# Delta-rule attention and MoE on one core: T K left out, transposes by halves of the rows, v and T straight beside crossed keys

## The chip, the cores and the metric

The kernel runs on one core of a Trainium2 chip. The metric is the device time of one execution in microseconds (us). Three runs of the kernel before took 693.31, 692.15 and 690.77 us; the median is 692.15.

## What is computed

The inputs are q, k and v (4 batches, 8 heads, 768 tokens, 48 numbers each), beta, and the weights of a two-layer MoE. Attention runs through the tokens with a state of 48 x 48 for each batch and head; its output, all heads of a token side by side (384 numbers), goes through the MoE. All is fp32.

```
for t in range(S):
    y[:, :, t] = einsum('bhd,bhde->bhe', q[:, :, t], state)
    v_old = einsum('bhde,bhd->bhe', state, kt)
    state = state + beta_t * einsum('bhd,bhe->bhde', kt, vt - v_old)
...
h = maximum(x @ w_in, 0)
out = (h * h) @ w_out
```

kt is k divided by its norm.

## The kernel before

**Units.** A unit is 128 tokens of two batches: two chunks (c) of 64 tokens, eight heads (h, as pairs p with j = 0 or 1 in a pair), two batches (b). There are 12 units (u). A tile has 128 partitions, 64 for each batch. Within a chunk the recurrence is solved in one go: with the products of keys K K' below the diagonal and beta a triangular matrix is inverted, and the inverse is T. If V and K are the chunk's values and keys and S the state before it, the chunk's update is U = T (V - K S). The state becomes S + K' U, and the output is Q S plus the masked products Q K' times U.

**Crosswise layout.** `load_to` (line 226) puts k, q and v so that the even heads of batch b lie in partition half b and the odd heads in the other half. `load_beta` lays beta in the same way (line 256). An operation on one half of the partitions then uses one half of TensorE's rows, and where the result lies sets the half of its columns: four quadrants of the array, which can work side by side.

**Stages of a unit.**
- `normalize`: k divided by its norm (ScalarE L273, VectorE L274 to L286).
- `static`: k and q are transposed on TensorE (L317, four 128x128 transposes for each chunk and each of k and q) and copied to `kq` by ScalarE (L318); products of keys with keys and queries (L327), masked by VectorE (L336); the key products go through DRAM into a layout for the inverse (`lt`).
- `invert`: 31 steps of two VectorE instructions (L415, L416) on `lt`, then DMAs through DRAM into `tt` (T) and `t1t`.
- `whole`: T's remaining quarter (L454, L462, copies L456, L466). Then, for both chunks, T K (L474), which is copied over the keys in `kq` (L483), and T V (L481), copied over `vt` (L484).
- `sequential`, for each chunk: (T K) S and Q S (L505), U = T V - (T K) S on VectorE (L508), K' U into the state (L518, L521), masked products times U (L526), copy of y (L529).
- `moe`: y is transposed (L541, three 128x128 for each chunk), split into a high part x_h (ScalarE, L543) and a low part x_l (VectorE, L544). Each product is made of three: high by high, high by low, low by high. First layer L574 into a PSUM bank `h` (nine matmuls make a step), activation L581, L582, cast L584 (h_h), low part on VectorE L553 (h_l); second layer L561 (six matmuls make a step) two groups behind the first.

**The order.** The code writes each engine's order itself. `weave` (line 613) interleaves the parts of one round by places between 0 and 1: the MoE of unit u-1 is the filler (34 steps), and between its steps come `static` of unit u+1, the state part (`whole` and `sequential`) of unit u in 7 steps from 0.34 to 0.98, the inverse of unit u+1, loads and norms. Each `yield` in a stage ends a step. Every engine takes its instructions in that order. The split of the weights into halves (`split_weights`) runs at the start and within unit 1.

**PSUM.** `ps_x` has two banks (transposes, products, T's parts, state updates), `ps_g` a pair of banks (chunk 1 of `static`, T V, the outputs of `sequential`), `ps_h` two (first layer, and the transposes of y), `ps_o` two (second layer).

Of the kernel before, what the change touches and what calls it, by code (L numbers as in the profile page):

```python
# [20 lines left out]
def kernel(  # L21
# [204 lines left out]
    def load_to(dst, x, d, width, queues=None):  # L226

        for j, queue in enumerate(queues or (nc.sync, nc.sync)):
            for b, src in enumerate(tokens(x, d)):
                rows = slice((b ^ j) * C, (b ^ j) * C + C)  # L230
                for c in range(NC):
                    queue.dma_start(out=dst[rows, c, j::2, :width], in_=src[:, c, j::2])

    def load(u):
        t0, b0 = (u // NU) * P, (u % NU) * 2
        d = dict(u=u, t0=t0, b0=b0, y=[None] * NC, marks={})
# [9 lines left out]
    def load_beta(d):  # L246
# [49 lines left out]
    def static(d):  # L296
# [15 lines left out]
        def transposed(c, which, bank=None):  # L312

            src = d["qp" if which else "kp"]
            tp = (x_tile(u) if bank is None else bank).rearrange("p (n t) -> p n t", n=NP)
            for p in range(NP):
                nc.tensor.transpose(tp[:, p], src[:, c, 2 * p:2 * p + 2].rearrange("p a b -> p (a b)"), ident)  # L317
            return lambda: nc.scalar.copy(out=kq[:, c, :, :, which], in_=tp.rearrange("p n (b t) -> p n b t", b=2))  # L318

        def products(c, first, n):  # L320

            ps = [x[:, :NP * n * C].rearrange("p (n t) -> p n t", n=NP) for x in banks(c)]
            for p in range(NP):
                for j in range(2):
                    rows = slice(j * C, j * C + D)
                    for b in range(2):
                        nc.tensor.matmul(ps[j][b * C:(b + 1) * C, p], lhsT=kq[rows, c, p, b, 0],  # L327
                                         rhs=kq[rows, c, p, b, first:first + n].rearrange("p x t -> p (x t)"),
                                         start=True, stop=True)
# [24 lines left out]
        if u <= 1:  # L354
            for c in range(NC):
                transposed(c, 0)()
                yield
# [7 lines left out]
            for c in range(NC):  # L365
                transposed(c, 1)()
                yield
# [9 lines left out]
        for copy in [transposed(c, which, bank) for c in range(NC) for which, bank in enumerate(banks(c))]:  # L377
            copy()
# [60 lines left out]
    def whole(d):  # L439

        u, ap, kp, vt, kq = (d[x] for x in ("u", "ap", "kp", "vt", "kq"))
# [26 lines left out]
        ps = [x_tile(u).rearrange("p (c n t) -> p c n t", c=NC, n=NP) for _ in range(2)]  # L468
        for c in range(NC):
            for h in range(H):  # L470
                p, j = h // 2, h % 2
                for b in range(2):
                    rows = slice(b * C, (b + 1) * C)
                    nc.tensor.matmul(ps[b][j * C:(j + 1) * C, c, p], lhsT=kp[rows, c, h], rhs=tt[rows, c, h],  # L474
                                     start=True, stop=True)
        g = ps_g.tile([P, 2, PC], F32, name="g")[:, :, :H * D].rearrange("p c (h e) -> p c h e", h=H)
        for c in range(NC):
            for h in range(H):
                for b in range(2):
                    rows = slice(b * C, (b + 1) * C)  # L480
                    nc.tensor.matmul(g[rows, c, h], lhsT=tt[rows, c, h], rhs=vt[rows, c, h], start=True, stop=True)  # L481
        for b in range(2):
            nc.scalar.copy(out=kq[:, :, :, b, 0], in_=ps[b])  # L483
        nc.scalar.copy(out=vt, in_=g)  # L484
        yield


    def sequential(d):
        u, s = d["u"], state[d["u"] % NU]
        kq, ap, kp, vt = (d[x] for x in ("kq", "ap", "kp", "vt"))  # L490
        for c in range(NC):
# [4 lines left out]
            if first:  # L496
                uu = vt[:, c]
            else:
# [267 lines left out]
```

## Time and profile before

| | |
|---|---|
| span of the profiled execution | 691.8 us |
| its place beside the runs | median of three runs 692.15 us, 0.35 above that span |
| TensorE matmuls (PE) | 628.9 us busy, 91% |
| weight loads (PEld, beside the matmuls) | 583.2 us, 84% |
| VectorE (DVE) | 433.1 us, 63% |
| ScalarE (ACT) | 332.8 us, 48% |
| GpSimd (POOL) | 76.4 us, 11% |
| DMA | 49.95 MB, 72 GB/s on average |

In the profile's rows a name such as `x<-tt,kpad` reads: written tile, then what is read, the moving operand ahead of the stationary one. A shape "64*64 64x48" is the weights' rows and columns, then the output. Busy times of matmuls are longer than the pace at which they follow each other, because they overlap; the pace is the difference of two start times. L numbers are lines of the kernel before; in the changed kernel the same statements stand some lines further down (L574 becomes L581, L561 L568, L553 L560, L317 L324, L327 L340, L505 L498, L518 L520, L526 L528, L481 L509, L508 L501, L541 L545, L544 L551, L415 and L416 L429 and L430).

### The profile page before, as it was taken

The numbers are of one execution on the slowest core, as the hardware profiler recorded it, in microseconds if no ns is written. First come the engines' busy times: TensorE is split into PE (matmuls) and PEld (weight loads), VectorE is DVE, ScalarE is ACT, GpSimd is POOL, SyncE is SP. The second block draws the span as 40 slices with busy tenths as digits, with TensorE's granted clock in tenths as the row PEclk, the third lists the DMA queues.
The fourth block names the chain that finished last, engine by engine and source line by source line (L and its number), as shares of the span: only waits on it lengthen the run. The fifth ranks groups of instructions, "written<-read, shape, count | busy, mean of one in ns | idle before, by whom it ended". The sixth has DMA issues, their size and how long they took to land.

```text
span 691.8 us, 23593 instructions
## 1 busy us (share of the span) xinstructions
PE 628.9 (91%) x10084; PEld 583.2 (84%) x10084; DVE 433.1 (63%) x1175; ACT 332.8 (48%) x632; POOL 76.4 (11%) x94
## 2 busy tenths in 40 slices
PE   1740797889999999999999999999999999999997
PEld 0530366779999999999999999999999999999997
DVE  3789776898468387477485494694674775641221
ACT  3630455763453544544535535535545445354352
POOL 8540332310100100001001001001000010000000
PEclk9985689999999999999999999999999999999999
DMA  7678620410441531532423414405315324030100
GB/s 158 158 207 290 195 48 5 91 24 2 89 81 20 103 67 23 107 55 39 96 48 55 99 28 77 90 17 114 65 18 107 58 36 97 3 61 3 24 2 23
DMA packets 174712, 49.95 MB, mean 72 GB/s; under 512 B 166400, under 2 KB 169488, under 8 KB 174608
## 3 DMA queue, kind: packets, MB, share of 16 engines
q1 hardware_dynamic: 172016, 47.85, 32.4%
q8 instruction: 79, 1.29, 0.8%
q10 hardware_dynamic: 2336, 0.59, 0.4%
q14 instruction: 25, 0.20, 0.1%
q0 software_dynamic: 256, 0.01, 0.1%
HBM read 37.32 MB, written 11.01 MB: 70 GB/s over the span
## 4 chain that ended last, share of the span: by engine, by line
PE 78%; DVE 4%; ACT 1%; issue 1%; DVEq 0%
PE h L574 30%; PE o L561 29%; PE g L505 3%; PE g L481 3%; PE x L518 2%; PE x L474 2%; PE x L327 2%; PE g L526 1%; PE g L327 1%; PE g L317 1%; PE x L317 1%; PE h L541 1%; PE x L462 1%; PE x L454 1%; DVE tmp L415 1%
## 5 line engine op out<-in xcount | busy, mean ns | idle before, releaser
L561 PE MATMUL o<-w,h_h 128*128 128x384 f32 x768 | 203.7, 346 | 0.0
L574 PE MATMUL h<-x_h,w 128*128 128x256 f32 x1152 | 173.4, 286 | 1.7 <-ACT x_h L543 1.7
L574 PEld LDWEIGHTS h<-x_h,w 128*128 128x128 f32 x1152 | 153.6, 189 | 7.3 <-ACT x_h L543 2.0
L553 DVE TENSOR_TENSOR h_l<-r,h_h 128x512 fp32r<-128x512 f32 x96 | 66.6, 694 | 147.9 <-PE o L561 61.5
L581 ACT ACTIVATE r<-h 128x512 f32<-128x512 f32 x96 | 57.5, 599 | 179.0 <-PE h L574 178.7
L561 PEld LDWEIGHTS o<-w,h_h 128*128 128x128 f32 x768 | 133.2, 188 | 2.4
L561 PE MATMUL o<-w,h_l 128*128 128x384 f32 x384 | 129.8, 338 | 0.0
L415 DVE SCALAR_TENSOR_TENSOR tmp<-lt,bt,z 128x126 f32<-128x126 f32 (+22 forms) x310 | 95.4, 308 | 22.7 <-DMA out_dram<-a 10.5
L574 PE MATMUL h<-x_l,w 128*128 128x256 f32 x576 | 99.8, 282 | 0.0
L416 DVE TENSOR_TENSOR z<-z,tmp 128x126 f32<-128x126 f32 (+22 forms) x310 | 79.2, 255 | 10.7
L574 PEld LDWEIGHTS h<-x_l,w 128*128 128x128 f32 x576 | 82.1, 190 | 0.0
L561 PEld LDWEIGHTS o<-w,h_l 128*128 128x128 f32 x384 | 72.2, 188 | 0.0
L582 ACT ACTIVATE r<-r 128x512 f32<-128x512 f32 x96 | 60.7, 632 | 3.0
L584 ACT CAST h_h<-r 128x512 fp32r<-128x512 f32 x96 | 59.5, 620 | 3.1
L399 POOL MEMSET z<- 128x512 f32 x10 | 5.3, 532 | 401.4 <-DMA inv<-z 355.0
L143 POOL TENSOR_SCALAR a<-a 128x384 f32<-128x384 f32 (+1 forms) x19 | 26.6, 1399 | 47.0 <-ACT a L142 46.8
L274 DVE TENSOR_REDUCE n<-rest 128x8 f32<-128x384 f32 x20 | 10.8, 549 | 31.5 <-ACT rest L273 31.5
L466 ACT ACTIVATE tt<-x 32x256 f32<-32x256 f32 x42 | 15.7, 375 | 26.3 <-PE x L462 25.8
L170 PE MATMUL o<-r,plus 128*128 128x512 f32 (+1 forms) x16 | 10.4, 737 | 19.8 <-DVE r L153 19.8
L543 ACT CAST x_h<-h 128x384 fp32r<-128x384 f32 x24 | 11.6, 482 | 32.2 <-PE h L541 32.2
L505 PEld LDWEIGHTS g<-state,kq 48*64 48x64 f32 x1408 | 22.5, 134 | 4.3 <-issue 2.8
L481 PE MATMUL g<-vt,tt 64*64 64x48 f32 x768 | 25.8, 223 | 0.0
(143 smaller groups left out, 774.2 us busy)
## 6 DMA issues: line engine op xcount, KB each, us to landing
w<-in_moe_w_in_dram SPq DMA_DIRECT2D x12, 512.0 KB
w<-in_moe_w_out_dram SPq DMA_DIRECT2D x16, 384.0 KB
lt<-blocks SPq DMA_DIRECT2D x22, 256.0 KB
vt<-in_v_dram SPq DMA_DIRECT2D x96, 48.0 KB
out_dram<-a SPq DMA_DIRECT2D x46, 96.0 KB
kpad<-in_k_dram SPq DMA_DIRECT2D x88, 48.0 KB
qpad<-in_q_dram SPq DMA_DIRECT2D x88, 48.0 KB
blocks<-ap SPq DMA_DIRECT2D x48, 64.0 KB
```

Of the source, the lines that this page charges most:

```text
L143: nc.gpsimd.tensor_scalar(out=a.bitcast(F32), in0=a.bitcast(F32), scalar1=LEAST, scalar2=None, op0=ALU.max)
L327: nc.tensor.matmul(ps[j][b * C:(b + 1) * C, p], lhsT=kq[rows, c, p, b, 0], rhs=kq[rows, c, p, b, first:first + n].rearrange("p x t -> p (x ...
L415: nc.vector.scalar_tensor_tensor(out=tmp, scalar=bt[:, s:s + 1], op0=ALU.mult, op1=ALU.mult, **factors)
L416: nc.vector.tensor_tensor(out=z[:, :nj, s + 1:], in0=z[:, :nj, s + 1:], in1=tmp, op=ALU.subtract)
L481: nc.tensor.matmul(g[rows, c, h], lhsT=tt[rows, c, h], rhs=vt[rows, c, h], start=True, stop=True)
L505: nc.tensor.matmul(dst[to * C:(to + 1) * C, j, p], lhsT=kq[rows, c, p, b, x], rhs=s[rows, b, p], start=(x == 0 and p == 0), stop=False, sk ...
L553: nc.vector.tensor_tensor(out=h_l, in0=r, in1=h_h.bitcast(F32), op=ALU.subtract)
L561: nc.tensor.matmul(o[i], lhsT=a[:, e, i * P:(i + 1) * P], rhs=halves["wo", ft][w], start=(ft == 0 and n == 0), stop=(ft == FT - 1 and n == 2))
L574: nc.tensor.matmul(hp[:, e], lhsT=halves["wi", (kt, ft // EACH)][w][:, f], rhs=x[:, kt], start=(n == 0), stop=(n == 3 * KT - 1))
L581: nc.scalar.activation(out=r, in_=hp, func=AF.Relu)
L582: nc.scalar.activation(out=r, in_=r, func=AF.Square)
L584: nc.scalar.copy(out=h_h, in_=r)
```

## The change

1. **No T K.** `whole` ends after T's remaining quarter. In `sequential` the state is multiplied by the untouched keys, VectorE subtracts K S from v in place (`vt`), and T is applied to the difference, chunk by chunk: 16 matmuls into two banks (`tv`), two ScalarE copies into `uu`. A chunk thus has one step more, except the first chunk of the first two units; the state part has 8 steps in place of 7. There is no copy over `kq` or over `vt` from PSUM any more.
2. **v, beta and T straight.** v and beta are loaded with batch b in half b for all heads: four DMAs each in place of eight. The key products of odd heads cross over to the other half (`to = 1 - b`), so that T lies straight; the query products stay. For odd heads one matmul of 128 columns becomes two of 64. K S crosses to the straight half (`to = b ^ j` for both products), and T's product crosses back to the crosswise half.
3. **Transposes by halves of the rows.** Each 128x128 transpose of k, q and y becomes two of 64 rows by 128 columns, one for each half of the partitions and each into its own PSUM bank. The copies out take one bank each: for k and q, one copy holds a half's keys and queries; for y, both chunks are transposed ahead of the two x_h copies and the two x_l subtractions.

The core of the diff:

```diff
@@ load_to
+        if x is v:
+            for b, src in enumerate(tokens(x, d)):
+                for c in range(NC):
+                    nc.sync.dma_start(out=dst[b * C:(b + 1) * C, c], in_=src[:, c])
+            return
@@ load_beta
         for n in range(4):
-            for j in range(2):
-                queue.dma_start(out=d["bt"][x + n * H2 + j:x + (n + 1) * H2:2], in_=by[n // 2 ^ j, n % 2][:, j::2])
+            queue.dma_start(out=d["bt"][x + n * H2:x + (n + 1) * H2], in_=by[n // 2, n % 2])
@@ static
-        def transposed(c, which, bank=None):
+        def transposed(parts, pair, into):
...
+            for x, (c, which) in enumerate(parts):
+                src = d["qp" if which else "kp"]
+                for p in range(NP):
+                    for b in range(2):
+                        rows = slice(b * C, (b + 1) * C)
+                        nc.tensor.transpose(pair[b][:, x, p], src[rows, c, 2 * p:2 * p + 2].rearrange("p a b -> p (a b)"),
+                                            ident[rows, rows])
+            for b in range(2):
+                nc.scalar.copy(out=into[:, :, :, b], in_=pair[b])
@@ products
+                    for x in range(first, first + n) if j else (first,):
+                        for b in range(2):
+                            to = b if x or not j else 1 - b
+                            m = 1 if j else n
...
@@ whole
-                    nc.tensor.matmul(ps[b][j * C:(j + 1) * C, c, p], lhsT=kp[rows, c, h], rhs=tt[rows, c, h],
...
-                    nc.tensor.matmul(g[rows, c, h], lhsT=tt[rows, c, h], rhs=vt[rows, c, h], start=True, stop=True)
-        for b in range(2):
-            nc.scalar.copy(out=kq[:, :, :, b, 0], in_=ps[b])
-        nc.scalar.copy(out=vt, in_=g)
-        yield
@@ sequential
-                                to = b ^ j if x else b
+                                to = b ^ j
...
+                left = vt[:, c].rearrange("p (n j) e -> p j n e", j=2)
+                nc.vector.tensor_tensor(out=left, in0=left, in1=gs, op=ALU.subtract)
+                yield
+            tv = [x_tile(u)[:, :NP * D].rearrange("p (n e) -> p n e", n=NP) for _ in range(2)]
+            for h in range(H):
+                p, j = h // 2, h % 2
+                for b in range(2):
+                    rows, to = slice(b * C, (b + 1) * C), slice((b ^ j) * C, ((b ^ j) + 1) * C)
+                    nc.tensor.matmul(tv[j][to, p], lhsT=tt[rows, c, h], rhs=vt[rows, c, h], start=True, stop=True)
+            uu = apool.tile([P, H, D], F32, name="r", bufs=2)
+            for j in range(2):
+                nc.scalar.copy(out=uu[:, j::2], in_=tv[j])
             yield
@@ moe
+                for b in range(2):
+                    rows = slice(b * C, (b + 1) * C)
+                    nc.tensor.transpose(xt[b][:, kt, i], y[rows, kt * P:(kt + 1) * P], ident[rows, rows])
+            if i == 0:
+                yield
+        for b in range(2):
+            at = [x.rearrange("p n (i b t) -> p n i b t", i=2, b=2)[:, :, :, b] for x in (x_h, x_l)]
+            nc.scalar.copy(out=at[0], in_=xt[b])
+            nc.vector.tensor_tensor(out=at[1], in0=xt[b], in1=at[0].bitcast(F32), op=ALU.subtract)
+        yield
@@ the rounds
-            parts.append((state_part(ds_[u]), 7, *Q1))
+            parts.append((state_part(ds_[u]), 8 - (u < NU), *Q1))
```

**What that does to the order.** First TensorE, in `whole` of a unit. Before, the two products (x and g are PSUM banks, tt is T, kpad the keys, o and h the MoE's banks):

```order
L561 MATMUL o_4605<-w_856,h_l 128x384
L561 MATMUL o_4606<-w_856,h_h 128x384 x2
L561 MATMUL o_4606<-w_856,h_l 128x384
L474 MATMUL x<-tt_110,kpad_104 64x64 x32
L481 MATMUL g<-vt,tt_110 64x48 x32
L574 MATMUL h<-x_h,w_1010 128x256
```

Now T's product for one chunk stands alone, between the two halves of a first-layer group and two filler steps behind that chunk's L498:

```order
L581 MATMUL h<-x_l,w_1011 128x256
L581 MATMUL h<-x_l,w_1060 128x256
L581 MATMUL h<-x_l,w_1096 128x256
L509 MATMUL x<-vt,tt_110 64x48 x16
L581 MATMUL h<-x_h,w_1011 128x256
```

The 64 matmuls in one place have become 16 in each of two places. Between L498 and L509 stand six L568 and nine L581.

TensorE again, where the last y is transposed and `static` of the next unit begins (plus is the identity, kpad and qpad are k and q). Before:

```order
L541 MATMUL h<-plus,y 128x128 x3
L317 MATMUL x<-plus,kpad_100 128x128 x4
L317 MATMUL x<-plus,qpad 128x128 x4
L317 MATMUL g<-plus,kpad_100 128x128 x4
L317 MATMUL g<-plus,qpad 128x128 x4
L574 MATMUL h<-x_h,w_373 128x256
```

Now:

```order
L545 MATMUL h<-plus,y 128x64 x6
L324 MATMUL x<-plus,kpad_100 128x64 x8
L324 MATMUL x<-plus,qpad 128x64 x8
L324 MATMUL g<-plus,kpad_100 128x64 x8
L324 MATMUL g<-plus,qpad 128x64 x8
L581 MATMUL h<-x_h,w_377 128x256
```

The place is the same, with twice as many transposes of half the columns.

Last VectorE, at the first chunk's subtraction (L508, now L501). Before, it comes behind a row of the norms (L274), an h_l and a pair of the inverse:

```order
L274 TENSOR_REDUCE n_5084<-rest 128x8
L553 TENSOR_TENSOR h_l<-r,h_h 128x512
L415 SCALAR_TENSOR_TENSOR tmp<-lt,bt,z 128x120
L416 TENSOR_TENSOR z<-z,tmp 128x6x20
L508 TENSOR_TENSOR r<-vt,g 128x2x4x48
L415 SCALAR_TENSOR_TENSOR tmp<-lt,bt,z 128x133
```

Now it stands six pairs of the inverse earlier, right behind the h_l of the group before, and the norms' row comes later:

```order
L429 SCALAR_TENSOR_TENSOR tmp<-lt,bt,z 128x78
L430 TENSOR_TENSOR z<-z,tmp 128x3x26
L560 TENSOR_TENSOR h_l<-r,h_h 128x512
L501 TENSOR_TENSOR vt<-vt,g 128x2x4x48
L429 SCALAR_TENSOR_TENSOR tmp<-lt,bt,z 128x100
L430 TENSOR_TENSOR z<-z,tmp 128x4x25
```

The second chunk's subtraction moved in the same way, to right behind an h_l.

More of the change, by code (lines that the diff above doesn't have):

```diff
@@ L310, in banks @@
             return [g[:, 0], g[:, 1]]
-        def transposed(c, which, bank=None):
[L314 to L318, printed above, removed]
+        def transposed(parts, pair, into):
+            pair = [x.rearrange("p (x n t) -> p x n t", x=2, n=NP) for x in pair]
+            for x, (c, which) in enumerate(parts):
[7 more added lines that the diff above has]
+                nc.scalar.copy(out=into[:, :, :, b], in_=pair[b])
         def products(c, first, n):
@@ L354, in static @@
         if u <= 1:
-            for c in range(NC):
-                transposed(c, 0)()
-                yield
+            yield
+            transposed([(c, 0) for c in range(NC)], [x_tile(u) for _ in range(2)], kq[:, :, :, :, 0])
+            yield
             for c in range(NC):
@@ L364, in static @@
             yield
-            for c in range(NC):
-                transposed(c, 1)()
-                yield
+            yield
+            transposed([(c, 1) for c in range(NC)], [x_tile(u) for _ in range(2)], kq[:, :, :, :, 1])
+            yield
             for c in range(NC):
@@ L376, in static @@
             return
-        for copy in [transposed(c, which, bank) for c in range(NC) for which, bank in enumerate(banks(c))]:
-            copy()
+        for c in range(NC):
+            transposed([(c, 0), (c, 1)], banks(c), kq[:, c].rearrange("p n b x t -> p x n b t"))
         yield
@@ L467, in whole @@
         yield
[L468 to L482, printed above, removed]
-            nc.scalar.copy(out=kq[:, :, :, b, 0], in_=ps[b])
-        nc.scalar.copy(out=vt, in_=g)
-        yield
     def sequential(d):
         u, s = d["u"], state[d["u"] % NU]
-        kq, ap, kp, vt = (d[x] for x in ("kq", "ap", "kp", "vt"))
+        kq, ap, kp, vt, tt = *(d[x] for x in ("kq", "ap", "kp", "vt")), ttile[u % 2]
         for c in range(NC):
@@ L495, in sequential @@
             gs, gy = [g[:, :, x * NP * D:(x + 1) * NP * D].rearrange("p j (n e) -> p j n e", n=NP) for x in range(2)]
-            if first:
-                uu = vt[:, c]
-            else:
+            if not first:
                 for x, dst in ((0, gs), (1, gy)):
@@ L536, in moe @@
         x_l = mpool.tile([P, KT, 2 * P], F32R, name="x_l", bufs=1)
+        xt = [ps_h.tile([P, PC], F32, name="h")[:, :KT * P].rearrange("p (n i t) -> p n i t", n=KT, i=2) for _ in range(2)]
         for i in range(2):
             y = d["y"][i].rearrange("p h e -> p (h e)")
-            xt = ps_h.tile([P, PC], F32, name="h")[:, :KT * P].rearrange("p (n t) -> p n t", n=KT)
             for kt in range(KT):
-                nc.tensor.transpose(xt[:, kt], y[:, kt * P:(kt + 1) * P], ident)
-            cols = slice(i * P, (i + 1) * P)
-            nc.scalar.copy(out=x_h[:, :, cols], in_=xt)
-            nc.vector.tensor_tensor(out=x_l[:, :, cols], in0=xt, in1=x_h[:, :, cols].bitcast(F32), op=ALU.subtract)
-            yield
+                for b in range(2):
+                    rows = slice(b * C, (b + 1) * C)
+                    nc.tensor.transpose(xt[b][:, kt, i], y[rows, kt * P:(kt + 1) * P], ident[rows, rows])
+            if i == 0:
+                yield
+        for b in range(2):
+            at = [x.rearrange("p n (i b t) -> p n i b t", i=2, b=2)[:, :, :, b] for x in (x_h, x_l)]
+            nc.scalar.copy(out=at[0], in_=xt[b])
+            nc.vector.tensor_tensor(out=at[1], in0=xt[b], in1=at[0].bitcast(F32), op=ALU.subtract)
+        yield
         o = [ps_o.tile([P, PC], F32, name=f"o{i}")[:, :DM] for i in range(2)]
```

18 lines of the change are left out of this document (8 added, 10 removed).

## Prediction

> **What bounds the kernel now.** I read the page first, then the busy time by stretches, then TensorE's instructions in order of time through one whole unit, with VectorE's beside them. The page's busy line and its TensorE slices:
>
> ```profile
> PE 628.9 (91%) x10084; PEld 583.2 (84%) x10084; DVE 433.1 (63%) x1175; ACT 332.8 (48%) x632; POOL 76.4 (11%) x94
> PE   1740797889999999999999999999999999999997
> ```
>
> TensorE's idle tenth lies in the first quarter. The stretches (length, then TensorE's busy time) show where that ends:
>
> ```profile
> 150.00:200.00 50.00, 47.49 (x762) 45.14 (x763) 33.09 (x98) 22.99 (x43) 1.96 (x3) 0.97 0.25 48
> 200.00:250.00 50.00, 50.00 (x903) 47.51 (x903) 31.68 (x94) 24.92 (x48) 1.95 (x3) 1.00 0.34 65
> ```
>
> From about 172 us TensorE never rests, so there a term of TensorE counts in full, unless another engine keeps it waiting. The unit that I cost is 318 to 367 us and the first part of the next (start, length, line, count; matmuls overlap, so I go from start to start; a plain fp32 matmul leaves two records):
>
> ```profile
> 318.01 0.96 PE L574 MATMUL h<-x_h,w 128*128 128x256 f32 x6
> ...
> 359.73 0.68 PE L518 MATMUL x<-r,kpad 64*64 64x48 f32 x32
> 360.23 0.65 PE L526 MATMUL g<-r,ap 64*64 64x48 f32 x32
> 360.81 0.62 PE L561 MATMUL o<-w,h_h 128*128 128x384 f32 x2
> ...
> 364.42 0.49 PE L541 MATMUL h<-plus,y 128*128 128x128 f32 x3
> 364.75 0.60 PE L317 MATMUL x<-plus,kpad 128*128 128x128 f32 x4
> ...
> 366.06 0.60 PE L317 MATMUL g<-plus,qpad 128*128 128x128 f32 x4
> 366.63 0.96 PE L574 MATMUL h<-x_h,w 128*128 128x256 f32 x6
> ...
> 371.03 1.10 PE L327 MATMUL x<-kq 48*64 48x128 f32 x32
> 371.96 1.05 PE L327 MATMUL g<-kq 48*64 48x128 f32 x32
> 372.94 0.98 PE L574 MATMUL h<-x_h,w 128*128 128x256 f32 x6
> ...
> 388.39 0.34 PE L561 MATMUL o<-w,h_l 128*128 128x384 f32 x1
> 388.66 1.16 PE L474 MATMUL x<-tt,kpad 64*64 64x64 f32 x64
> 389.64 2.03 PE L481 MATMUL g<-vt,tt 64*64 64x48 f32 x64
> 391.60 0.97 PE L574 MATMUL h<-x_h,w 128*128 128x256 f32 x6
> 393.82 0.52 PE L561 MATMUL o<-w,h_h 128*128 128x384 f32 x2
> ...
> 394.98 1.15 PE L505 MATMUL g<-state,kq 48*64 48x48 f32 x64
> 396.06 0.62 PE L561 MATMUL o<-w,h_h 128*128 128x384 f32 x2
> 397.22 0.87 PE L574 MATMUL h<-x_h,w 128*128 128x256 f32 x6
> ```
>
> A unit lasts 366.63 - 318.01 = 48.62 us. Going back from 318.01 by three of them gives 172.2; forward from 366.63 by five, 609.7, where the chain of waits has the first h group that no transposes of k and q interrupt:
>
> ```profile
> 608.77 6.51 PE h L574 x54
> ```
>
> So nine periods count in full; one without inverse or transposes of k and q follows, then the last MoE.
>
> **Removed: T times K, and T times v's place.** L474's 64 records take 0.98 us (15.3 ns each), L481's 1.96 us (30.6 ns). With 0.09 us to enter (388.39 plus one L561 matmul, 0.18, against 388.66) both go from 388.57 to 391.60: **-3.03**.
>
> **Added: T's product, twice.** Each half has 32 records that go through all four quadrants of the array. L518 and L526 are such blocks: 64 records from 359.73 to 360.81, 15.6 ns each and 0.08 to leave. So each new block is 32 x 15.6 ns = 0.50 plus 0.17 for entry and exit, 0.67; two are **+1.34**. The other bound is L481's pace, which used two quadrants: 2 x (0.98 + 0.17) = 2.30. I take the first, since L526 writes its two row halves into banks in the same way as the new product will. The Trainium skill (TensorEngine Tiling (Array Packing), Gotcha 1: PSUM Pressure) says that different row tiles cannot access one PSUM bank at once; by that the sum would hold 2.30. L526's 15.6 ns speaks against it.
>
> **The key products.** L327 takes 1.91 us. Half of its matmuls are cut into two of half the width: 96 records in place of 128-column ones, the same columns in each quadrant. With four quadrants at work, a 128-column record keeps its quadrant for 4 x 1.91/64 = 119 ns, and two of 64 columns for 2 x 4 x 15.3 = 122: **+0.1**. At most the 32 more records cost 15.6 ns each, +0.5.
>
> **The transposes by halves.** L317's 16 full transposes go at (366.06 - 364.75)/12 = 0.109 us each, 1.74, and L541's six, 0.65: 2.39 in all. Now 44 halves stand there, in two groups that enter and leave a smaller tile shape (2 x 0.17 = 0.34). No row shows a half. How long its weight load is decides (minimum, median, maximum ns):
>
> ```profile
> L454 PEld LDWEIGHTS x<-tt,ap x704: 101/104/108, 78.7 to 620.0; 32*32 32x32 f32 x176
> L481 PEld LDWEIGHTS g<-vt,tt x768: 135/135/223, 88.7 to 630.3; 64*64 64x64 f32 x192
> L574 PEld LDWEIGHTS h<-x_h,w x1152: 186/188/333, 109.3 to 680.0; 128*128 128x128 f32 x192
> L317 PEld LDWEIGHTS x<-plus,kpad x52: 139/140/230, 12.3 to 559.6; 128*128 128x128 f32 x52
> ```
>
> 32, 64 and 128 columns take 104, 135 and 188 ns, but a transpose's 128 columns only 140, near the 64-column load. So I take a pair of halves, which use different rows and banks, at about L481's pair (61 ns), 64 ns: 22 x 0.064 + 0.34 = 1.75, **-0.64**. If a pair lasts as long as a full transpose: 22 x 0.109 + 0.34 = 2.74, +0.35. If halves follow one another at 0.109 each: 5.14, +2.75. The Trainium skill (TensorE: Matmul & The Clock Gate, LDWEIGHTS) states that a load takes its columns divided by 1.2 in ns, however many rows: an estimate of 107 ns for 128 columns, so that halving the rows saves nothing and the +0.35 would hold. The three steps 104, 135, 188 agree with it; the transposes' 140 does not.
>
> TensorE's work thus falls by 3.03 - 1.34 - 0.1 + 0.64 = 2.23 us a unit. The rest is whether it may go that much faster.
>
> **The waits that this adds.** The subtraction on VectorE used to have three filler steps before TensorE needed it; now T's product follows after two, and VectorE has an h_l ahead of it. VectorE's rows (idle time before them in brackets):
>
> ```profile
> 347.77 0.55 DVE L274 TENSOR_REDUCE n<-rest 128x8 f32<-128x384 f32 x1 [3.40 <-ACT rest L273]
> 348.80 0.69 DVE L553 TENSOR_TENSOR h_l<-r,h_h 128x512 fp32r<-128x512 f32 x1 [0.47 <-PE o L561]
> 349.41 0.34 DVE L415 SCALAR_TENSOR_TENSOR tmp<-lt,bt,z 128x120 f32<-128x120 f32 x1
> 349.98 0.55 DVE L508 TENSOR_TENSOR r<-vt,g 128x384 f32<-128x384 f32 x1
> 350.44 0.35 DVE L415 SCALAR_TENSOR_TENSOR tmp<-lt,bt,z 128x133 f32<-128x133 f32 x1
> 354.66 0.68 DVE L553 TENSOR_TENSOR h_l<-r,h_h 128x512 fp32r<-128x512 f32 x1
> 365.94 1.01 DVE L544 TENSOR_TENSOR x_l<-h,x_h 128x384 fp32r<-128x384 f32 x2
> 385.98 0.25 DVE L415 SCALAR_TENSOR_TENSOR tmp<-lt,bt,z 128x31 f32<-128x31 f32 x1 [1.59 <-DMA out_dram<-a]
> 397.42 0.69 DVE L553 TENSOR_TENSOR h_l<-r,h_h 128x512 fp32r<-128x512 f32 x1 [0.47 <-PE o L561]
> ```
>
> The inverse's first step (128x31) in another unit, and that unit's first h matmuls:
>
> ```profile
> 220.63 0.96 PE L574 MATMUL h<-x_h,w 128*128 128x256 f32 x6
> ...
> 241.52 0.25 DVE L415 SCALAR_TENSOR_TENSOR tmp<-lt,bt,z 128x31 f32<-128x31 f32 x1 [3.06 <-DMA out_dram<-a]
> ```
>
> h_l waits until its buffer's last L561 matmuls end: 397.42, 0.20 after the next group starts at 397.22. In the new order nine h matmuls (1.06: eighteen lie between 391.60 and 393.82 with the 0.1 of a re-entry) stand between that point and T's product, which could start at 1.06 + 0.09 = 1.15. VectorE needs 0.20 + 0.61 (h_l) + 0.55 (subtraction) + about 0.05 to signal = 1.41. So each of T's products waits about 0.26: **+0.5 a unit**. At the first of the two, VectorE comes from the inverse, whose first step waits for a DMA: it begins 385.98 - 366.63 = 19.35 after the unit's h matmuls in one unit and 20.89 in the other. How much of that reaches T's product no row of before shows: between nothing and 20.89 - 19.35 = 1.54. I take **+0.15**, near nothing, because VectorE still had 3.40 idle (347.77) between these steps and its next duty.
>
> **The second gate.** L574's first matmul needs the bank that the first x_l frees: 365.94 + 0.55 (1.01 for the two, which overlap; one as L508, of the same size) = 366.49, and it starts at 366.63. No row of VectorE from 348.80 to there has idle time in brackets, so TensorE already just waits for VectorE at that point. Count from the relu group before, P = 393.82 - 48.62 = 345.20. TensorE's part from P to 366.63 loses L505's first block (1.17 with entry), gains one of T's products (0.67), the transposes' -0.64 and a wait of 0.26: it could end 0.9 earlier. VectorE can't follow: its second h_l (354.66, P + 9.46) would come 0.47 + 0.46 earlier by its queue (the wait at 348.80 goes and the first subtraction, 349.98 to 350.44, leaves this stretch), but its buffer is now freed at P + 2.12 + 1.17 + 2.12 + 1.06 + 1.17 + 1.06 + 0.20 = P + 8.90 (twelve L561, L518 and L526, eighteen L574, six L561, L505, six L561). So x_l comes 0.56 earlier, not 0.9. The other part of the unit changes by -3.03 + 1.17 + 0.67 + 0.1 + 0.26 + 0.15 = -0.68. Together **-1.24 a unit**, of the 2.23 saved.
>
> ScalarE loses three copies of the old products and gains four of 128x192. A copy of twice that size takes 0.48:
>
> ```profile
> 360.95 0.48 ACT L529 COPY y<-g 128x384 f32<-128x384 f32 x1 [1.32 <-PE g L526]
> ```
>
> Two take less than 0.96, and 1.06 + 2.12 us of filler stand between T's product and their reader, so I cost them at nothing; without that cover it is those 0.96. SyncE issues four DMAs fewer each for v and beta; nothing on the path waits for those. The two x_h copies now stand together behind the last transposes, but x_l is later than they are.
>
> **The sum.** Nine periods: -11.2. The last one: -3.03 + 1.34 + 0.5 and 0.1 for the y halves, -1.1. Before 172 us the start waits for VectorE and DMAs; both chunks' transposes now come ahead of the first copy, +0.3. Total -12.0 on a span of 691.8; the median of the runs is 692.15, 0.35 above the span: **680 us**.
>
> **The rivals.**
> - *Half transposes are no faster as pairs.* TensorE's second part then ends at -1.17 + 0.67 + 0.35 + 0.26 = +0.1, past VectorE's gate; a unit gains 0.58: nine are -5.2, with the ends -6: **686**. For it: the load rows above; against: the 140 ns.
> - *The waits don't come* (h_l finds its buffer early, x_l isn't the gate): 9 x 2.23 + 1 = 21: **671**. Against it: VectorE's unbroken rows up to 365.94.
> - *VectorE's queue gates every unit.* If the inverse starts as late everywhere as in the other unit, each first subtraction is late by 1.54, of which 0.15 are in the sum: -1.24 + 1.39 = +0.15, nine are +1.4, with the ends +0.6: **693**. For it: VectorE's 63% sits in the very stretch in which the new waits lie.
> - *Slower: halves one after another.* With +2.75 a unit goes to -0.68 - 1.17 + 0.67 + 2.75 + 0.26 = +1.83; nine are +16.5: **709**. It decides from (2.39 + 0.92 - 0.34)/44 = 68 ns a half on. Against it: L474's 15.3 ns, which needs both row halves to work at once on the same columns.
>
> **How the numbers follow.** Forecast 0.42; even pairs 0.20; no waits 0.13; gated 0.15; halves in series 0.10. The range leaves out the last and half of the third: 672 to 693. A change within 0.5% is about what a measurement of this kernel can't tell from none (the three runs spread by 0.4%). Faster by more, 0.75: the first three; the same, 0.15: the gated case; slower, 0.10: the last.
>
> **What would show it.** Right: T's product as two blocks of 0.5 us that each start about 0.25 late; the four groups of k and q transposes at about 1.0 us instead of 1.74; the first h matmul behind them waiting on x_l; a period near 47.4. Wrong: transposes above 1.7 us; a period under 46.8, with no gap ahead of T's product; or VectorE idle ahead of x_l.

## The result and the profile after

| | median, us (runs) | range |
|---|---|---|
| before | 694.83 (20) | 690.77 to 700.32 |
| after | 691.58 (20) | 688.23 to 694.77 |

The ratio of after to before is 0.9947 (95% interval 0.9926 to 0.9967): 0.5% faster, where the prediction had 1.7%. The profiled execution of after has a span of 691.2 us. In the kernels of the experiments some line numbers shift by a few, up to ten (the first h matmuls, L581 here, are L582 with h_l later).

The page's busy line and TensorE's slices:

```profile
PE 612.2 (89%) x9900; PEld 557.1 (81%) x9900; DVE 435.6 (63%) x1175; ACT 322.8 (47%) x644; POOL 75.1 (11%) x90
PE   0850887879999999999999999999999999999997
```

TensorE is busy 16.7 us less than before (628.9), but the span is shorter by 0.6. The busy time by stretches says where the difference went: most of it is now idle time in the steady part. From 174 to 608 us TensorE is busy 422.04 of 434.00, where before had no idle time at all. For 200 to 250 us, where before has 50.00 of 50.00 busy, after has:

```profile
200.00:250.00 50.00, 48.34 (x840) 45.28 (x839) 33.08 (x99) 23.33 (x48) 1.96 (x3) 1.00 0.33 64
```

TensorE's rows of one unit of after, in order of time, show where it waits:

```profile
367.45 0.94 PE L581 MATMUL h<-x_h,w 128*128 128x256 f32 x6 [0.51 <-ACT kq L327]
...
391.53 0.51 PE L581 MATMUL h<-x_l,w 128*128 128x256 f32 x3
392.51 0.79 PE L509 MATMUL x<-vt,tt 64*64 64x48 f32 x32 [0.47 <-DVE tmp L429]
393.24 0.97 PE L581 MATMUL h<-x_h,w 128*128 128x256 f32 x6
...
394.40 0.51 PE L568 MATMUL o<-w,h_h 128*128 128x384 f32 x2
...
404.77 0.68 PE L509 MATMUL x<-vt,tt 64*64 64x48 f32 x32 [0.26 <-DVE vt L501]
405.38 0.97 PE L581 MATMUL h<-x_h,w 128*128 128x256 f32 x6
...
413.71 0.40 PE L545 MATMUL h<-plus,y 64*128 64x64 f32 x6
413.95 0.42 PE L324 MATMUL x<-plus,kpad 64*128 64x64 f32 x8
414.20 0.41 PE L324 MATMUL x<-plus,qpad 64*128 64x64 f32 x8
...
415.64 0.94 PE L581 MATMUL h<-x_h,w 128*128 128x256 f32 x6 [0.53 <-DVE x_l L551]
```

The brackets show three waits in each unit: 0.47 and 0.26 at T's two products, 0.53 at the first h matmul, 1.26 together. (A bracket counts from the end of the matmul before, which is modelled; part of a wait can lie ahead of that end.) The unit lasts 415.64 - 367.45 = 48.19. The eight units from 173.86 to 560.95 last 48.39 on average (48.19 to 48.90; the long ones have up to 1.10 at the first of T's products), against 48.66 before: -0.27 a unit, where the prediction had -1.24.

VectorE's rows of the same unit:

```profile
368.70 0.69 DVE L432 TENSOR_TENSOR z<-z,bt 128x512 f32<-128x512 f32 x1
...
387.00 0.25 DVE L429 SCALAR_TENSOR_TENSOR tmp<-lt,bt,z 128x31 f32<-128x31 f32 x1 [1.64 <-DMA lt<-blocks]
...
391.10 0.69 DVE L560 TENSOR_TENSOR h_l<-r,h_h 128x512 fp32r<-128x512 f32 x1 [0.74 <-PE o L568]
391.71 0.55 DVE L501 TENSOR_TENSOR vt<-vt,g 128x384 f32<-128x384 f32 x1
392.17 0.32 DVE L429 SCALAR_TENSOR_TENSOR tmp<-lt,bt,z 128x100 f32<-128x100 f32 x1
...
403.56 0.69 DVE L560 TENSOR_TENSOR h_l<-r,h_h 128x512 fp32r<-128x512 f32 x1 [0.39 <-PE o L568]
404.17 0.55 DVE L501 TENSOR_TENSOR vt<-vt,g 128x384 f32<-128x384 f32 x1
404.63 0.34 DVE L429 SCALAR_TENSOR_TENSOR tmp<-lt,bt,z 128x126 f32<-128x126 f32 x1
...
414.95 1.01 DVE L551 TENSOR_TENSOR x_l<-h,x_h 128x384 fp32r<-128x384 f32 x2
```

Each subtraction (L501) stands behind an h_l (L560) that VectorE cannot begin before TensorE has left its buffer (L568). From 404.63 to x_l at 414.95 no row has idle time in brackets: VectorE works without a gap, and x_l comes when its queue comes to it.

The theory from this: TensorE's saving is given back because VectorE's order holds it, first with h_l ahead of the subtraction, then with x_l at the end of an unbroken row. One rival: the smaller tile shapes themselves cost what was saved. Another: the loss lies ahead of 172 us.

### The profile page after: what moved, and what is told of

The parts are those of the page before. It is cut to its first block, busy times and chain, and to the rows that moved or that the text cites. A ratio compares the mean times of both kernels' runs of the same rounds, so it can differ in the third digit from the quotient of the medians.

```text
span 691.2 us, 23095 instructions
## 1 busy us (share of the span) xinstructions
PE 612.2 (89%) x9900; PEld 557.1 (81%) x9900; DVE 435.6 (63%) x1175; ACT 322.8 (47%) x644; POOL 75.1 (11%) x90
## 5 line engine op out<-in xcount | busy, mean ns | idle before, releaser
L568 PE MATMUL o<-w,h_h 128*128 128x384 f32 x768 | 204.7, 348 | 0.0
L581 PE MATMUL h<-x_h,w 128*128 128x256 f32 x1152 | 176.2, 289 | 7.5 <-DVE x_l L551 6.1
L560 DVE TENSOR_TENSOR h_l<-r,h_h 128x512 fp32r<-128x512 f32 x96 | 66.6, 694 | 155.6 <-PE o L568 70.4
L581 PEld LDWEIGHTS h<-x_h,w 128*128 128x128 f32 x1152 | 154.6, 191 | 11.8 <-ACT kq L327 5.6
L568 PEld LDWEIGHTS o<-w,h_h 128*128 128x128 f32 x768 | 133.2, 189 | 3.3
L568 PE MATMUL o<-w,h_l 128*128 128x384 f32 x384 | 130.1, 339 | 0.0
L581 PE MATMUL h<-x_l,w 128*128 128x256 f32 x576 | 100.2, 283 | 0.0
L581 PEld LDWEIGHTS h<-x_l,w 128*128 128x128 f32 x576 | 82.8, 191 | 0.0
L568 PEld LDWEIGHTS o<-w,h_l 128*128 128x128 f32 x384 | 72.6, 189 | 0.0
L512 ACT COPY r<-x 128x192 f32<-128x192 f32 x46 | 12.6, 324 | 72.2 <-PE x L509 72.2
L498 PEld LDWEIGHTS g<-state,kq 48*64 48x64 f32 x1408 | 23.3, 138 | 5.5 <-issue 5.5
L509 PEld LDWEIGHTS x<-vt,tt 64*64 64x64 f32 x736 | 15.4, 134 | 13.3 <-issue 8.4
L498 PE MATMUL g<-state,kq 48*64 48x48 f32 x1408 | 26.1, 224 | 0.0
```

Of the source, the lines that this page charges most:

```text
L498: nc.tensor.matmul(dst[to * C:(to + 1) * C, j, p], lhsT=kq[rows, c, p, b, x], rhs=s[rows, b, p], start=(x == 0 and p == 0), stop=False, sk ...
L509: nc.tensor.matmul(tv[j][to, p], lhsT=tt[rows, c, h], rhs=vt[rows, c, h], start=True, stop=True)
L512: nc.scalar.copy(out=uu[:, j::2], in_=tv[j])
L560: nc.vector.tensor_tensor(out=h_l, in0=r, in1=h_h.bitcast(F32), op=ALU.subtract)
L568: nc.tensor.matmul(o[i], lhsT=a[:, e, i * P:(i + 1) * P], rhs=halves["wo", ft][w], start=(ft == 0 and n == 0), stop=(ft == FT - 1 and n == 2))
L581: nc.tensor.matmul(hp[:, e], lhsT=halves["wi", (kt, ft // EACH)][w][:, f], rhs=x[:, kt], start=(n == 0), stop=(n == 3 * KT - 1))
```

## The experiments

They were run in three groups, each beside the kernel before (medians of before 694.52 us for the first four rows, 693.52 for the next four, 693.60 for the last four). Runs of different groups are best compared by their ratios. "Period" is that of the steady units in the one profiled execution.

| run | median, us | ratio to before (95%) | period, us |
|---|---|---|---|
| h_l later | 678.05 | 0.9754 (0.9724 to 0.9784) | 47.08, three units 47.8 to 48.5 |
| inverse behind x_l | 701.76 | 1.0098 (1.0070 to 1.0126) | 47.9 and 51 to 52 by turns |
| both | 692.24 | 0.9971 (0.9948 to 0.9994) | 47.4 and 49 to 51 by turns |
| full transposes | 687.46 | 0.9889 (0.9864 to 0.9914) | 48.25, one unit 49.24 |
| before, halves alone | 697.09 | 1.0050 (1.0028 to 1.0071) | 48.63 |
| before, h_l later | 690.76 | 0.9932 (0.9901 to 0.9963) | 48.41 |
| full at the start alone | 689.78 | 0.9935 (0.9902 to 0.9968) | 48.26 |
| h_l later, full | 675.01 | 0.9717 (0.9683 to 0.9751) | 47.12 to 47.35 |
| h_l later, y as before | 676.86 | 0.9758 (0.9722 to 0.9795) | 47.12, two units 47.4 |
| y as before | 686.65 | 0.9904 (0.9867 to 0.9942) | 48.22 |
| h_l later, gap filled | 675.37 | 0.9734 (0.9697 to 0.9772) | 47.08, one unit 47.68 |
| all three | 672.76 | 0.9714 (0.9672 to 0.9756) | 47.08, two units 47.3 and 47.8 |

**h_l later.** In `second`, the h_l that waits for a buffer is put behind the matmuls that free it:

```diff
-                rest()
+                if e:
+                    rest()
                 yield
```

> The changed kernel, but each h_l is emitted behind the second half of its L568 step and not behind the first, so that on VectorE the subtraction (L501) stands ahead of the h_l that waits for TensorE's L568. Theory (VectorE's order gives the saving back): of the 1.24 us that TensorE waits in a unit (0.47 and 0.26 at T's product, 0.51 at the first h matmul), both waits at T's product go; x_l comes only about 0.4 earlier, because VectorE's row is full from there on, so a wait of some 0.4 stays at the first h matmul. Period 48.4 -> about 47.4, nine units -8: about 684 us, 0.984 of before. Rival A (the small tile shapes themselves cost what was saved, the waits are only where the slack shows): the period stays within 0.2 of 48.4 and the waits come up elsewhere, 690 to 692. Rival B (what is lost is lost before 172 us, in the unit with the weight split): the periods may fall, but the first unit with a MoE stays 4 us longer than before, and the time stays above 688.

VectorE's rows of one unit, and TensorE's:

```profile
382.28 0.55 DVE L501 TENSOR_TENSOR vt<-vt,g 128x384 f32<-128x384 f32 x1
...
383.27 0.68 DVE L560 TENSOR_TENSOR h_l<-r,h_h 128x512 fp32r<-128x512 f32 x1
...
405.97 1.01 DVE L551 TENSOR_TENSOR x_l<-h,x_h 128x384 fp32r<-128x384 f32 x2
```

```profile
359.58 0.95 PE L582 MATMUL h<-x_h,w 128*128 128x256 f32 x6 [0.35 <-DVE x_l L551]
...
383.66 0.51 PE L582 MATMUL h<-x_l,w 128*128 128x256 f32 x3
384.10 0.68 PE L509 MATMUL x<-vt,tt 64*64 64x48 f32 x32
384.71 0.98 PE L582 MATMUL h<-x_h,w 128*128 128x256 f32 x6
...
406.67 0.94 PE L582 MATMUL h<-x_h,w 128*128 128x256 f32 x6 [0.32 <-DVE x_l L551]
```

The subtraction now ends at 382.83, and T's product begins at 384.10 with no wait. x_l comes 405.97 - 359.58 = 46.39 into the unit, where it came at 414.95 - 367.45 = 47.50 in after. The period is 47.09, 1.1 less from one moved instruction; on the average of the eight units it is 47.43 against 48.39, the 1.0 of the theory. Rival A (the tile shapes) is out: the waits at T's products vanish in the ordinary units and do not come up elsewhere. The time falls by 13.5 us, more than the expected 8. In the profiled executions 7.7 of it are in the eight units and 2.0 behind them. The other 4.0 lie ahead of the steady part, and 3.5 of these ahead of the first MoE, where the two programs are the same: the first h matmul came at 107.06 in after and at 103.53 here. So that much is a difference between two executions, and this experiment does not show it to come from h_l.

**The inverse behind x_l**, and both edits together:

```diff
-                parts.append((inverse, NI - n_i, 0, I1 - 1, "quiet"))
+                parts.append((inverse, NI - n_i, 0.08, I1 - 1, "quiet"))
```

> The changed kernel, but two of the inverse's steps that stand ahead of x_l on VectorE stand behind it (1.0 us of VectorE). Theory: x_l comes up to 1.0 earlier, the wait of 0.51 at the first h matmul goes, the two at T's product (0.73 and more) stay: period 48.4 -> about 47.8, nine units -5: about 687 us, 0.988 of before. Rival A (tile shapes): the period stays within 0.2. A third way: the inverse ends later and T's DMAs keep L468 waiting, which would show as a wait there of up to 1 us.

> Both edits together. Theory: no wait is left on TensorE, the period is its own work, 48.2 - 1.24 = 46.95 against 48.6 before: nine units -13 against the changed kernel, about 679 us, 0.977 of before. Rival A (tile shapes): 690 to 692. Rival B (the start): periods of 47, but 684 or more, the rest lost ahead of 172 us.

Both were wrong. x_l did come earlier (the wait for it falls to 0.23 to 0.25, now for the x_h copy that x_l itself needs), but every other unit lasts 2 to 4 us longer. VectorE's rows of such a unit of the run with the inverse behind x_l, whose first h matmul starts at 222.40, then SyncE's queue and TensorE's rows:

```profile
224.79 0.56 DVE L603 COPY a<-o 128x384 f32<-128x384 f32 x1
225.27 0.68 DVE L432 TENSOR_TENSOR z<-z,bt 128x512 f32<-128x512 f32 x1
...
244.85 0.25 DVE L429 SCALAR_TENSOR_TENSOR tmp<-lt,bt,z 128x31 f32<-128x31 f32 x1 [4.55 <-DMA lt<-blocks]
```

```profile
226.01 1.27 SPq L436 DMA_DIRECT2D inv<-z  x2
231.14 1.91 SPq L445 DMA_DIRECT2D tt<-inv  x4
...
235.16 2.78 SPq L358 DMA_DIRECT2D blocks<-ap  x4
239.67 1.15 SPq L366 DMA_DIRECT2D lt<-blocks  x2
```

```profile
249.53 0.69 PE L509 MATMUL x<-vt,tt 64*64 64x48 f32 x28 [2.57 <-DVE tmp L429]
```

z is finished at 225.27 + 0.68, 3.55 into the unit (in after 1.25 + 0.69 = 1.94), because two more steps of the inverse and a copy (L603) now come between x_l and it. Its DMAs open a chain on one queue, SyncE's: out, back as T, then the next unit's blocks, out and back as lt. So the next inverse starts late (244.85, 22.45 into the unit; 19.55 in after), and the subtraction stands behind its first steps: T's product waits 2.57. This chain is read from rows; it was not tested by itself. In the units between, z began just as late (2.87 into the unit, in both), but the same DMAs landed sooner (z to the next inverse 17.2 in place of 19.6) and the wait stayed at 0.47; why the units alternate stays open. After has slow DMAs in its long units too. SyncE's queue there, for an ordinary unit (367.45) and a long one (222.12):

```profile
232.77 2.00 SPq L358 DMA_DIRECT2D blocks<-ap  x4
238.18 1.14 SPq L366 DMA_DIRECT2D lt<-blocks  x2
...
378.22 2.00 SPq L358 DMA_DIRECT2D blocks<-ap  x4
381.86 1.14 SPq L366 DMA_DIRECT2D lt<-blocks  x2
```

From the blocks' issue to the issue of their way back it takes 5.4 in the long unit and 3.6 in the ordinary one.

**Full transposes in the changed kernel.** Only the transposes go back; the copies behind them keep their number and size:

```diff
-                for p in range(NP):
-                    for b in range(2):
-                        rows = slice(b * C, (b + 1) * C)
-                        nc.tensor.transpose(pair[b][:, x, p], src[rows, c, 2 * p:2 * p + 2]..., ident[rows, rows])
+                for p in range(NP):
+                    nc.tensor.transpose(pair[x][:, p], src[:, c, 2 * p:2 * p + 2]..., ident)
...
-                    nc.tensor.transpose(xt[b][:, kt, i], y[rows, kt * P:(kt + 1) * P], ident[rows, rows])
+                nc.tensor.transpose(xt[i][:, kt], y[:, kt * P:(kt + 1) * P], ident)
```

> The changed kernel with all transposes of k, q and y as full 128x128 ones again; the rest of the change stays, its copies keep their size. TensorE's work rises by the 2.45 - 1.73 = 0.72 that the rows show, less 0.18 for two entries into the smaller shape. Theory: this falls into the wait for x_l (0.51), so the period rises by 0.0 to 0.15 and the time by 0 to 1.5 us, and the wait at the first h matmul goes. Rival (what the transposes save counts): +0.54 a unit, +5 us, about 696.5.

TensorE's first h matmuls of one unit and the next:

```profile
360.64 0.95 PE L576 MATMUL h<-x_h,w 128*128 128x256 f32 x6
...
408.87 0.96 PE L576 MATMUL h<-x_h,w 128*128 128x256 f32 x6
```

The period is about 48.25 in seven of eight units (48.23 here), and the bracket at the first h matmul is gone: as the theory had it, what the halves saved had only become waiting for x_l. The time did not stay but fell, to 687.46, and that is not in the units: see the start, below.

**The halves alone, in the kernel before**, and **h_l later, in the kernel before**. The first takes the change's transposes (L317 and L541 become L324 and L545) with the copies behind them; the second is the `if e:` above.

> The kernel before with one part of the change: the transposes of k, q and y by halves of the rows; T times K and all else stay. TensorE's work falls by the same 0.54 us a unit. Theory (x_l on VectorE starts each MoE, TensorE is just on time there): nothing comes of it, a wait of about 0.5 for x_l appears at the first h matmul, period 48.6 as before, 693 to 696 us; up to 4 us more if the halves also cost time in the start. Rival (transposes are TensorE's work and count): -0.54 a unit, -5 us, about 690.

> The kernel before with the one edit of the earlier run that put h_l behind the subtraction on VectorE, and nothing else. Theory: TensorE waits nowhere in a unit of before, its work sets the period, so 48.6 stays and the time is 692 to 696 us; h_l's place matters only together with the change. Rival (the order on VectorE is worth this by itself): -1 us a unit or more, 685 or less.

The run with the halves has TensorE done with its transposes earlier, and waiting:

```profile
368.57 0.42 PE L320 MATMUL g<-plus,qpad 64*128 64x64 f32 x8
369.50 0.95 PE L584 MATMUL h<-x_h,w 128*128 128x256 f32 x6 [0.51 <-DVE x_l L554]
...
418.14 0.94 PE L584 MATMUL h<-x_h,w 128*128 128x256 f32 x6 [0.52 <-DVE x_l L554]
```

418.14 - 369.50 = 48.64: the period of before to 0.02, with the new wait of 0.51. The rival is out. The run with h_l later missed by a little: the period falls to 48.41, though no row of before has a wait. Its rows at the end of the transposes show why:

```profile
360.18 0.60 PE L317 MATMUL g<-plus,qpad 128*128 128x128 f32 x4
360.54 0.95 PE L575 MATMUL h<-x_h,w 128*128 128x256 f32 x6
...
408.95 0.95 PE L575 MATMUL h<-x_h,w 128*128 128x256 f32 x6
```

From the last four transposes to the first h matmul it takes 0.36 here and 0.57 in before (366.06 to 366.63 in the prediction's rows). So before does wait 0.2 for x_l, hidden in the step from one row to the next. But 0.2 is all that h_l's place is worth without the change, and 1.1 with it.

**Full transposes with h_l later:**

> The changed kernel with h_l behind the subtraction, and full transposes everywhere. With h_l later the steady period was 47.08 with 0.32 of waiting for x_l. Theory: full transposes add 0.54 of work, of which 0.32 go into that wait: period 47.3, +2 us against 678, unless the start gains the 4 us that full transposes gave without the edit: 676 to 680. Rival (transposes never matter because VectorE sets the period): the period stays at 47.1 and the wait goes.

The period is 47.1 to 47.3 without a wait, against 47.08 in the ordinary units of h_l later with 0.32 of waiting: there the halves are worth some 0.1 a unit. On the average of eight units it is the other way round, 47.18 against 47.43, because the run with h_l later has three long units.

**The start.** Full transposes gained 4.1 us in the changed kernel, and the halves alone cost before 3.6, with average periods equal to 0.1 in both pairs. With h_l later full transposes gained 3.0, but there 2.0 are in the units' average, and the intervals of the two ratios overlap. Three runs look for the place. The first has full ones where `u <= 1`:

```diff
+            if u <= 1:
...
+                        nc.tensor.transpose(one[:, p], src[:, c, 2 * p:2 * p + 2]..., ident)
```

> The changed kernel with full transposes of k and q for the first two units alone; from the third on halves, as in the change. If what full transposes everywhere gained (about 4 us, none of it in the steady periods) comes from the first two units' transposes, this gives 687 to 688 us. If it comes from elsewhere ahead of 172 us (the order of the split unit, when TensorE's clock falls there), it stays at 690 to 692. The steady periods stay at 48.2 to 48.6 with the same waits in both cases.

The other two have y and x as before:

```diff
-                    nc.tensor.transpose(xt[b][:, kt, i], y[rows, kt * P:(kt + 1) * P], ident[rows, rows])
...
+                nc.tensor.transpose(xt[:, kt], y[:, kt * P:(kt + 1) * P], ident)
+            cols = slice(i * P, (i + 1) * P)
+            nc.scalar.copy(out=x_h[:, :, cols], in_=xt)
```

> The changed kernel with nothing but the transposes of y and the copies of x as in the kernel before. Theory: first unit 63 in place of 66.8, steady periods as they were, 48.2 to 48.6 with the same waits: 687 to 688.5 us. Rival (start not from there): 690 to 692.

> The changed kernel with h_l behind the subtraction (678 us), and with the transposes of y and the copies of x as in the kernel before: full transposes, the first chunk's copy ahead of the second chunk's transposes. k and q keep their halves. Theory (the halves lose ahead of 172 us through one gap: TensorE waits 2.9 us for x_h and x_l ahead of the first h matmul, where it waited 2.3 with full ones and 1.7 before, and its granted clock then falls to 0.5 for three windows more): the gap goes to 2 or less, the first unit with a MoE shortens from 66.3 to about 63, and the time falls by 3 to 4 us, to 674.5. The steady period stays at 47.1, since VectorE's x_l holds it, or falls by up to 0.2. Rival (the start's loss comes from the k and q halves, or by chance): the first unit stays at 66, 677 to 678.

None settles it. Full transposes of k and q in the first two units give 689.78, whose interval holds after's. y as before gives 686.65, but its first unit with a MoE is as long as in after (66.84), though the gap ahead of it has shrunk from 2.90 to 1.89; with h_l later it gives 676.86 and a first unit of 64.79. The theory of the one gap fell. What the first unit's length does go with is the granted clock. In the fourteen profiles the unit takes 60.5 us where its mean clock is 0.97, 62.7 to 62.8 at 0.95, 63.6 to 64.1 at 0.92, and 64.8 to 66.8 at 0.85 to 0.89. Its first 18 us (the third number from the right is the clock) in before, in after, with h_l later (and the first 3 of them), with the gap filled, and with all three edits:

```profile
109.28:127.28 18.00, 15.16 (x145) 13.96 (x145) 13.14 (x24) 9.85 (x18) 4.44 (x3) 0.91 0.22 47
```

```profile
107.06:125.06 18.00, 15.31 (x160) 14.54 (x161) 10.74 (x21) 8.23 (x16) 2.65 (x2) 0.73 0.14 26
```

```profile
103.53:121.53 18.00, 15.88 (x158) 14.75 (x159) 10.49 (x20) 7.94 (x15) 2.65 (x2) 0.64 0.10 16
103.53:106.53 3.00, 3.00 (x14) 3.00 (x15) 2.73 (x6) 0.57 (x1) 1.17 (x1) 0.50 0.02 5
```

```profile
104.05:122.05 18.00, 15.34 (x168) 14.57 (x168) 11.78 (x22) 9.36 (x18) 3.26 (x3) 0.81 0.25 51
```

```profile
105.70:123.70 18.00, 15.33 (x201) 14.31 (x204) 13.82 (x25) 11.14 (x20) 5.54 (x4) 1.00 0.26 50
```

The filled runs have these extra matmuls:

```diff
+        if d["u"] == 0:
+            for _ in range(16):
+                nc.tensor.matmul(o[0], lhsT=plus, rhs=halves["wo", 0][0], start=True, stop=True)
```

> The changed kernel with h_l behind the subtraction, and 16 extra matmuls of 128x384 (about 2.9 us) behind the last transposes ahead of the first MoE's h matmuls, where TensorE has nothing to do but wait; their result is overwritten. If the clock is lost because TensorE idles there, the granted clock behind that place stays at 1.0, the first unit falls from 66.3 to 62 or 63, and the time from 678 to 674 to 675 although there is more work. If the clock has other causes, or the unit is long for other reasons, the time stays at 677 to 679.

> All three together: h_l behind the subtraction, y and x as before, and the 16 extra matmuls in the gap. If gap and clock are the cause in both, the two do not add up: 673 to 675 us, the first unit at 62 to 63, and steady periods of 47.1. If they are two causes they add: 670 to 671.

In 18 us a clock of 0.91 loses 1.62 us of TensorE, 0.73 loses 4.86, 0.64 loses 6.48, 0.81 loses 3.42 and 1.00 nothing. The first h matmuls of two runs, with h_l later, then with the gap filled:

```profile
103.53 1.62 PE L582 MATMUL h<-x_h,w 128*128 128x256 f32 x6 [2.87 <-DVE x_l L551]
```

```profile
104.05 0.95 PE L585 MATMUL h<-x_h,w 128*128 128x256 f32 x6
```

Six matmuls take 1.62 behind a gap of 2.87 and 0.95 behind one filled with work that nobody needs. But the length of the gap alone does not decide. Behind 1.89 the first six took 1.65 with y as before and 0.97 with h_l later too; behind 2.31, with full transposes, 0.95. After the same gap of 2.9 the clock of the first 18 us was 0.64 in one execution, 0.73 in another and 0.81 in a third. Nor did the filled gap bring what was expected of it: the first unit took 64.99, not 62 to 63, for TensorE waits again a little later (by 108.8 us), and the clock falls behind that wait.

By the ratios the filled runs are 0.2% (0.9754 to 0.9734) and 0.4% (0.9758 to 0.9714) faster, but the intervals of each pair overlap: the clock in the rows is shown, its worth in time and what sets it off are not. The losses come in steps of about 1.7. Counted from 3 us ahead of the first h matmul, where the clock is 0.92 in after and 0.88 with h_l later, they are 5.10 and 6.84, three and four times 1.7; the 3.42 with the gap filled is two times that, and the 1.62 of before once. At half clock (the 0.50 above) 1.7 is the loss of 3.4 us. The Trainium skill (TensorE: Matmul & The Clock Gate, Part 1) gives just such a free-running window of about 3.4 us, after which the clock halves; these steps agree with it. Its Part 4 says that the full clock doesn't engage for transposes, which don't count as busy in the same way; the stretch ahead of the first MoE is transposes and waiting, which fits, but no run here separates the two. Which of the halves brings the start its loss stays open.

The version with all three edits, 672.76 us, is the fastest of all; with h_l later and full transposes it is 675.01, and their intervals overlap.

## Why the prediction was wrong

The direction was right, and so were the mechanisms: T's product waits for the subtraction behind an h_l, x_l gates the next unit, the transposes go in pairs. The size was not: -3.3 us in the medians instead of -12. The spans of the two profiled executions differ by -0.6, so there 11.4 of the -12.0 are missing: 7.8 in the eight steady units (-0.27 instead of -1.24 each), 1.3 in the ninth (47.40 before, 47.45 after), 0.7 behind it and 1.6 ahead of them all.

**The steps that failed** are the two places where TensorE meets VectorE's queue. In the ordinary unit above (48.19 against 48.62) -0.43 came of the -1.24; of the missing 0.81, 0.44 lie ahead of the relu group (the second-layer matmuls that start at 394.40) and 0.37 behind it. The long units add 0.16 to the average.

- *Ahead: T's first product with its wait, 0.67 + 0.41.* This part changed by (394.40 - 367.45) - (393.82 - 366.63) = -0.24 and not by -0.68. Three L581 matmuls from 391.53 take 0.35, so the product with its wait lasts from 391.88 to 393.24, and the return to full-size matmuls takes 0.10 more: 1.46, not 1.08. The h_l began 0.27 and not 0.20 behind the start of the next group (390.83). The product began 0.25 and not 0.05 behind the subtraction's end (392.26), and its block lasted 0.73 and not 0.61. The bracket names the inverse's step behind the subtraction, which ends at 392.49; why the product waits for that, and why its block is slower, no run shows.
- *Behind: "So x_l comes 0.56 earlier".* Counted from the relu group, x_l came at 365.94 - 345.20 = 20.74 in before and 414.95 - 394.40 = 20.55 in after: **0.19 earlier**. The buffer of the h_l ahead of it came free at 403.56 - 394.40 = 9.16 and not at 8.90, since the list of blocks ahead of it left out two returns from small tiles to full-size matmuls (0.10 and 0.11) and took h_l to start 0.20 and not 0.27 behind the next group. From there to x_l VectorE needed 11.39, and 11.28 in before. The unit can't start its next MoE sooner than that queue lets it: the run with full transposes gave TensorE some 0.35 us of work back, and the period of the ordinary units rose by less than 0.1.

**TensorE's work, -2.23:** too large as well. Before works 48.41 in a unit, which is its period with h_l later, where nothing waits; the other 0.2 is the hidden wait for x_l. The changed kernel works 47.09 - 0.32 = 46.77, by the run with h_l later: -1.64. What after does not gain of that are its waits: 48.19 - 46.77 = 1.42 a unit, where the prediction had 2.23 - 1.24 = 0.99. By its terms:

- **T times K, and T V's place, -3.03:** right; after has none of it.
- **T's product, +1.34:** near. Without a wait a block takes 0.09 to enter (383.66 + 0.35 = 384.01, then 384.10) and 0.61 (to 384.71): 1.40 for two. **The pace** in four quadrants held; the 2.30 did not come that the Trainium skill's rule on one PSUM bank would give (TensorEngine Tiling (Array Packing), Gotcha 1: PSUM Pressure).
- **The key products, +0.1:** right, 1.91 became 2.03.
- **The transposes, -0.64:** a pair of halves takes 63 ns, near the forecast 64 (eight halves in 0.25, from 413.95 to 414.20), so the rival of even pairs is out. But 0.2 of what had stood under the full transposes (2.46 with the step to the first h matmul) was the hidden wait for x_l, and the halves of y enter the smaller shape twice (0.09 each): now 1.16 for k and q, 0.57 for y and 0.18, 1.91 against 2.26, **-0.35**.

With one more return to full-size matmuls (0.10) these terms make -1.76, 0.1 more than the -1.64 above; that 0.1 stays open.

What the prediction drew from the Trainium skill (TensorE: Matmul & The Clock Gate, LDWEIGHTS), that halving the rows saves nothing, holds for one load: that of a half takes 140 ns (the median below), as that of a full transpose does in the prediction's rows. The saving comes from two halves side by side:

```profile
L324 PEld LDWEIGHTS x<-plus,kpad x104: 136/140/222, 12.4 to 559.4; 64*128 64x128 f32 x104
```

**The waits at T's product, 0.26 and 0.41:** 0.26 and 0.47 by the brackets, up to 1.10 in the long units; from row to row, with 0.09 to enter, 0.34 and 0.54.

The rival "VectorE's queue gates every unit" came near in its number, 693 against 691.58, but that is luck. Its mechanism was an inverse that starts 20.89 into every unit and makes each first product 1.54 late. In five of the eight units the inverse started 19.4 to 19.9 into the unit; only in the three long ones was it 20.6 to 21.1, with waits of 0.65 to 1.10. With h_l behind the subtraction the same change gives 678.05, about the forecast (680); that is luck too, since the waits that the forecast had priced are gone there.

**The start, +0.3:** first h matmul 2.2 earlier than before (107.06 to 109.28), the first unit with a MoE 4.1 longer (66.80 to 62.73): in the profiled runs +1.9 together. The clock was not in the sum at all. One execution of each is little to go by here: the same code came to its first h matmul at 107.06 and at 103.53.

## What to carry to other kernels

Before pricing work taken off the busiest engine, find for each of its meeting points with an in-order engine how long that one's queue is unbroken ahead of it; what is saved beyond that slack becomes waiting. Then look in that queue for an instruction that waits for a buffer and stands ahead of one that the busy engine needs: moving it cost one line here and was worth more than three times the change itself (the ratio went from 0.9947 to 0.9754). Moving work later in such a queue is no mirror image of that, if its result opens a chain of DMAs.

## What the runs showed of the hardware

- A small-tile block takes 0.09 us to enter (384.01 to 384.10), and the first six full-size matmuls behind it take 0.1 longer than others (0.81 in place of 0.70: 393.24 to 394.05, against 390.83 to 391.53, in after).
- Two transposes of 64 rows and 128 columns (fp32), on different rows and banks, run as a pair in 63 ns, against 109 for one of 128 rows; the weight load of a half takes as long as that of a full one (140 ns both).
- A wait of 0.2 us behind transposes showed in no bracket, only in the step between two rows (0.57 in place of 0.36).
- Behind gaps of 1.9 to 2.9 us between matmuls the next six took between 0.95 and 1.65 us, from execution to execution; behind a gap filled with extra matmuls they took 0.95 and 0.87.
